# Batch 0 of x loaded and folded whole, the first half of w_in loaded in quarters, and the odd DFT units ahead of the even ones

## The chip, the cores and the metric

The kernel runs on one core of one Trainium2 chip. The metric is the time on the device in microseconds (us), the median of several executions. The kernel before took 1268.69 us (3 runs, 1268.38 to 1270.33). All runs told here gave correct results, and all their profiled executions were of the fast state, with a mean granted TensorE clock of 0.986 to 0.996.

Engines: PE is TensorE (PEld its weight loads), DVE is VectorE, ACT is ScalarE, POOL is GpSimd, SP is SyncE, which only issues DMAs here. SPq and ACTq are the queues in which SP and ACT issue them.

## The reference

```python
def reference(x, w_in, conv_w, w_out):          # x: 8 x 3136 x 256; w_in: 256 x 1024; w_out: 1024 x 256
    x = np.fft.fft(np.fft.fft(x, axis=1), axis=2).real.astype(np.float32)
    h = np.maximum(x @ w_in, 0.0)
    # three taps along the sequence, zero padded
    conv_out = sum(conv_w[k] * hp[:, k:k + S, :] for k in range(3))
    return ((h / (1.0 + np.exp(-conv_out))) @ w_out).astype(np.float32)
```

(Shortened.) The weights come as 64-bit floats and are narrowed to 32 bits on DVE.

## The kernel before

The sequence transform is cut down by symmetry. A *fold* on DVE (`pair`, `both`, `feats`, `evens`) adds and subtracts mirrored rows of x and leaves `w`. PE multiplies `w` with two cosine and sine tables in nine *units* (four even, two `odd_even`, two `odd`, one feature unit); each unit is copied from PSUM by ACT and finished by DVE (`fin`) into `pt` and `qt`. The transform along the feature axis is multiplied into w_in: `blocks` makes `G` from w_in and the DFT matrix `dm`. The main loop then makes `pa` and `pb` from `pt`, `qt` and `G`, and `combine` (DVE) starts the gated part. Row `er` is one row that goes by DMA from `qt` to one partition, through the feature unit on POOL, to DRAM (`ed`), and back in four broadcasts (`eb`); ACT *seeds* every `pa` from `eb`.

Only batch 0 has its fold and its transform in the open. For the other seven they are spread over the main loop.

How a weight is narrowed and where its raw bits lie:

```python
    def narrow(dst, raw):                       # seven DVE instructions
        lo, hi = raw[:, :, 0], raw[:, :, 1]
        ts(out=d, in0=hi, scalar1=20, scalar2=0x7FF, op0=lsr, op1=ALU.bitwise_and)
        # ... four more
        stt(out=lof, in0=lo.bitcast(U32), scalar=2.0 ** -32, in1=hi, op0=ALU.mult, op1=ALU.add)
        stt(out=dst, in0=lof, scalar=2.0 ** -20, in1=dst, op0=ALU.mult, op1=ALU.mult)
    class Weight:
        # self.raw = pool.tile([P, c, n, 2], I32, ...)    c: the two row halves t of w_in, n: columns
        def load(self, eng, c=None):
            eng.dma_start(out=self.raw[:, c].rearrange("p c n e -> p c (n e)"), in_=self.src[:, c])
        def narrow(self, c, cols):
            narrow(self.dst[:, c, cols], self.raw[:, c, cols])
```

The order of the head (cut):

```python
    w_cv.load(nc.scalar)
    nc.scalar.dma_start(out=dm, in_=dft_dim[:, :, 0:2])
    # x of batch 0 in two halves of 2 KB pieces, the second held back; then
    load_tables(1)                              # first table; w_in half 0, load_tables(0), w_in half 1 follow
    # ...
    for f in fold_ops(0): f()
    w_out.load(nc.sync)                         # its raw bits take x's buffer
    for par in (1, 0): mend_tables(par, half)   # ACT
    for i, u in enumerate(us[j] for j in (0, 1, 4, 2, 3, 5, 6, 7, 8)):   # 0, 1: odd, sn = 1; 5, 6: odd, sn = 0
        u.matmuls(0, 1); u.copy()               # PE; ACT
        if i == 2: flip()
        u.fin()                                 # DVE
        if i < 2: w_in[0].narrow(i, slice(0, H))
        if i == 1: row()                        # asks for er
        if i == 2: store(); spread(0, range(len(chunks)))   # ed; eb. Then x of batch 1
        if i == 6: blocks(0)
```

(In the list, 0 and 1 are the first `odd_even` and `odd`, 4 is the feature unit, 5 and 6 are the other `odd_even` and `odd`, and 2, 3, 7 and 8 are even.)

## Time and profile before

| | kernel before |
|---|---|
| median | 1268.69 us |
| span and clock of the profiled run | 1265.7 us, 0.994 |
| fold of batch 0 ends, w_out issued | 31.05, 23.05 us |
| `er` asked for, feature unit on POOL done | 47.25, 52.54 us |
| first seed, `combine` 0, `combine` 1 | 59.30, 62.24, 67.86 us |

The page of the profile gives the busy time of each engine as a share of the span, and then one digit per fortieth of the span (9 is 90% busy or more):

```profile
PE 1186.2 (94%) x4878; PEld 891.4 (70%) x4878; DVE 1146.4 (91%) x1739; ACT 885.4 (70%) x1835; POOL 397.9 (31%) x503
...
PE   0877999899999999999999999999999999999998
...
DVE  6499998999999989899899989998999878899996
```

PE is nearly full all along, but for the first slice of 31.6 us, with digit 0. What this change can win lies in and right after it. The prediction shows the other views of this kernel.

### The profile page before, as it was taken

The page shows a single profiled execution, that of the slowest core. Times are in us where ns is not written, and L with a number is a line of the kernel's source. Part 1 is how long each engine was busy: PE and PEld are TensorE (multiplying, and loading weights), DVE is VectorE, ACT ScalarE, POOL GpSimd, SP SyncE. Part 2 cuts the span into 40 slices and gives each one's busy share as a digit, 9 for nine tenths or more (in the row PEclk, how much of TensorE's full clock was granted, in tenths as well). Part 3 has the DMA queues.
Part 4 walks back from the last instruction along what each step waited for, and adds up shares of the span by engine and source line. Part 5 has one row for each costly group of instructions (what it writes and reads, how often), then busy time and mean ns, then how long its engine had stood idle before and what let it go on. Part 6 is the DMA issues. An engine that isn't in the chain of part 4 may idle for free.

```text
span 1265.7 us, 15557 instructions
## 1 busy us (share of the span) xinstructions
PE 1186.2 (94%) x4878; PEld 891.4 (70%) x4878; DVE 1146.4 (91%) x1739; ACT 885.4 (70%) x1835; POOL 397.9 (31%) x503
## 2 busy tenths in 40 slices
PE   0877999899999999999999999999999999999998
PEld 0545677677677767777677777777777777777776
DVE  6499998999999989899899989998999878899996
ACT  1344667677767767777767777776777778788885
POOL 5202642424333234242523324242322213222222
PEclk9988999999999999999999999999999999999999
DMA  9401321202212003020202103020011001010000
GB/s 238 146 16 30 98 77 45 58 28 75 64 58 68 26 22 95 25 84 26 72 24 64 49 26 91 31 83 1 26 45 33 30 26 38 28 29 30 30 26 30
DMA packets 47178, 66.06 MB, mean 52 GB/s; under 512 B 5684, under 2 KB 35276, under 8 KB 47096
## 3 DMA queue, kind: packets, MB, share of 16 engines
q1 hardware_dynamic: 41668, 51.93, 13.5%
q0 software_dynamic: 5120, 12.85, 3.7%
q8 instruction: 39, 0.64, 0.2%
q10 hardware_dynamic: 308, 0.29, 0.1%
q14 instruction: 43, 0.35, 0.1%
HBM read 39.26 MB, written 25.74 MB: 51 GB/s over the span
## 4 chain that ended last, share of the span: by engine, by line
PE 62%; DVE 23%; issue 5%; DMA 4%; ACT 4%; POOL 1%; SPq 0%; DVEq 0%; ACTq 0%; POOLq 0%
PE po L91 38%; PE pb L91 9%; PE pa L91 8%; DVE g L568 7%; PE pd L91 6%; DVE h L556 3%; DVE g L589 3%; DMA tab<-dft_seq_dram 2%; ACT nb L545 2%; DVE xh L158 1%; DVE xh L169 1%; DVE w L185 1%; ACT g L581 1%; DMA er<-qt 1%; DVE w L186 1%
## 5 line engine op out<-in xcount | busy, mean ns | idle before, releaser
L91 PE MATMUL po<-wout,g 128*128 128x256 f32 x3072 | 715.4, 382 | 32.4 <-DVE g L589 28.7
L91 PEld LDWEIGHTS po<-wout,g 128*128 128x128 f32 x3072 | 579.0, 190 | 194.5 <-DVE g L589 71.5
L568 DVE SCALAR_TENSOR_TENSOR g<-h,cw,g 128x770 f32<-128x770 f32 (+1 forms) x512 | 554.8, 1084 | 10.6 <-ACT g L562 1.5
L588 POOL TENSOR_TENSOR g<-g,h 128x385 f32<-128x385 f32 (+1 forms) x256 | 239.2, 935 | 743.5 <-ACT g L581 528.7
L581 ACT ACTIVATE g<-g 128x385 f32<-128x385 f32 (+2 forms) x512 | 244.5, 528 | 222.2 <-DVE g L568 222.0
L545 ACT ACTIVATE nb<-pb 128x386 f32<-128x386 f32 (+2 forms) x484 | 213.6, 494 | 83.0 <-PE pb L91 81.6
L556 DVE CUSTOM_DVE_ANT_0 h<-pa,nb 128x386 f32<-128x386 f32 (+2 forms) x498 | 258.2, 558 | 1.9 <-ACT h L542 1.9
L562 ACT ACTIVATE g<-h,cw 128x770 f32<-128x770 f32 (+1 forms) x256 | 243.6, 952 | 0.2 <-DVE h L556 0.2
L91 PE MATMUL pb<-qt,G 127*128 127x387 f32 (+2 forms) x512 | 213.9, 498 | 0.8 <-ACT nb L540 0.8
L91 PE MATMUL pa<-pt,G 128*128 128x387 f32 (+2 forms) x512 | 212.1, 495 | 0.9 <-ACT pa L513 0.5
L513 ACT ACTIVATE pa<-eb,ge 128x387 f32<-128x387 f32 (+2 forms) x256 | 154.0, 602 | 1.6 <-DVE h L556 1.6
L589 DVE TENSOR_TENSOR g<-g,h 128x385 f32<-128x385 f32 (+1 forms) x256 | 152.0, 594 | 1.2 <-ACT g L581 1.2
L91 PEld LDWEIGHTS pa<-pt,G 128*128 128x128 f32 x512 | 96.6, 189 | 75.4 <-issue 18.7
L91 PE MATMUL pd<-tab,w 99*128 99x196 f32 (+2 forms) x448 | 117.4, 374 | 0.0
L91 PEld LDWEIGHTS pb<-qt,G 127*128 127x128 f32 x512 | 94.0, 190 | 23.4 <-issue 3.5
L133 POOL DMA_INDIRECT xh<-in_x_dram,idx x64 | 98.1, 1533 | 17.9 <-issue 12.4
L91 PEld LDWEIGHTS pd<-tab,w 99*128 99x128 f32 (+1 forms) x448 | 82.9, 190 | 12.8
L608 ACT COPY os<-po 128x256 f32<-128x256 f32 x196 | 58.1, 397 | 10.4 <-PE po L91 5.8
L158 DVE TENSOR_TENSOR xh<-xh 98x1020 f32<-98x1020 f32 (+1 forms) x32 | 45.5, 1421 | 7.4 <-DMA xh<-in_x_dram,idx 7.4
L91 PE MATMUL po<-tab,w 98*128 98x196 f32 (+4 forms) x64 | 18.2, 442 | 26.6 <-ACT tab L223 23.7
L169 DVE TENSOR_TENSOR xh<-xh 98x1024 f32<-98x1024 f32 (+1 forms) x32 | 40.5, 1266 | 0.1
L91 PEld LDWEIGHTS po<-tab,w 98*128 98x128 f32 (+1 forms) x64 | 13.1, 222 | 30.6 <-issue 26.0
(100 smaller groups left out, 398.2 us busy)
## 6 DMA issues: line engine op xcount, KB each, us to landing
out_dram<-os SPq DMA_DIRECT2D x192, 128.0 KB
xh<-in_x_dram SPq DMA_DIRECT2D x16, 784.0 KB
eb<-ed SPq DMA_DIRECT2D x16, 193.5 KB
tab<-dft_seq_dram SPq DMA_DIRECT2D x4, 601.8 KB
raw<-in_moe_w_in_dram SPq DMA_DIRECT2D x2, 1024.0 KB
raw<-in_moe_w_out_dram SPq DMA_DIRECT2D x1, 2048.0 KB
eb<-ed SPq DMA_DIRECT2D x8, 209.0 KB
eb<-ed SPq DMA_DIRECT2D x8, 193.0 KB
```

The source lines that it names most:

```text
L91: nc.tensor.matmul(o, l, r, start=start, stop=stop, skip_group_check=True)
L133: nc.gpsimd.indirect_dma_start(out=xh[b, h][0:NP, 7 - m].rearrange("p q d -> p (q d)"), out_offset=None, in_=bass.AP(tensor=x.tensor, offs ...
L158: vt(a[:, :, :, 1:D], a[:, :, :, 1:D], r[:, :, :, D - 1:0:-1], op=ALU.add)
L513: act(pa[s][:, 0:n], eb[b, c], AF.Copy, scale=ge[:, f:f + 1])
L545: act(nb[s][:, i, cols], p[:, cols], AF.Copy, scale=-1.0 if i else 1.0)
L556: nc.vector._custom_dve(TENSOR_ADD_SAT, out=to, in0=a[:, cols], in1=c[:, i, cols], s0=BIG, s1=0.0)
L562: act(gs[s], hs[s][:, 0:n], AF.Copy, scale=cw[:, 0, s[2]:s[2] + 1])
L568: stt(out=g, in0=h[:, k:k + n], scalar=cw[:, k, f:f + 1], in1=g, op0=ALU.mult, op1=ALU.add)
L581: act(gs[s][:, c], gs[s][:, c], AF.Sigmoid)
L588: gt(g[:, p], g[:, p], h[:, p], op=ALU.mult)
L589: vt(g[:, v], g[:, v], h[:, v], op=ALU.mult)
L608: nc.scalar.copy(out=osb[:, j % 2], in_=pt[:, j % 2])
```

## The change

It has three parts, all in that head. Batch 0 of x comes in 4 KB pieces into one tile and is folded whole instead of in two halves. w_in is narrowed in quarters of 256 columns (quarters 0 and 1 come in one load each, quarters 2 and 3 in one together), and quarter 0 is loaded ahead of x, so that its narrowing and `blocks(0)` are done while x is on its way. The two odd units with sn = 0 go ahead of the even ones, and the mend of the second table is put off until they are through, so that nothing waits for that table. w_out's raw bits now lie in x's single tile, so its load follows the whole fold.

```diff
-    xp = ctx.enter_context(tc.tile_pool(name="xp", bufs=2))
+    xp = ctx.enter_context(tc.tile_pool(name="xp", bufs=1))
@@ class Weight
-        def load(self, eng, c=None):
-                eng.dma_start(out=self.raw[:, c].rearrange("p c n e -> p c (n e)"), in_=self.src[:, c])
+        def load(self, eng, cols=None):
+                eng.dma_start(out=self.raw[:, :, cols].rearrange("p c n e -> p c (n e)"),
+                              in_=self.src[:, :, 2 * cols.start:2 * cols.stop])
@@ loads
+    w_in[0].load(nc.sync, quarter(0))
     w_cv.load(nc.scalar)
+    zero(0, 0, nc.scalar)
     nc.scalar.dma_start(out=dm, in_=dft_dim[:, :, 0:2])
+    for m in (0, 2):
+        plain(0, 0, nc.sync, m, m + 2)
+    for m in range(4):
+        mirrored(0, 0, m)
+    load_tables(1)
+    w_in[0].load(nc.sync, quarter(1))
+    load_tables(0)
+    w_in[1].load(nc.sync)
@@ compute
     w_cv.narrow(0, slice(0, P))
+    narrow_in(0)                       # t = 0 and t = 1 of quarter 0
     for f in fold_ops(0):
         f()
     w_out.load(nc.sync)
-    for par in (1, 0):
-        mend_tables(par, half)
+    blocks(0)
+    mend_tables(1, half)
-    for i, u in enumerate(us[j] for j in (0, 1, 4, 2, 3, 5, 6, 7, 8)):
+    for i, u in enumerate(us[j] for j in (0, 1, 5, 6, 4, 2, 3, 7, 8)):
+        if i == 4:
+            mend_tables(0, half)
```

(Cut: the functions that address x, the other quarters, the loop that places them, and a part: ahead of `blocks(0)`, PE now multiplies the DFT matrix into the two `pa` buffers, with results that nothing reads. Before, `blocks(0)` itself used these buffers.)

More of the change, by code (lines that the diff above doesn't have):

```diff
@@ L95, in spare @@
         return pso.tile([P, 2, D], F32, name="po", tag="po").rearrange("p a d -> p (a d)")
-    xh, wt, ea = {}, {}, {}
-    idx = const.tile([P, 1], I32, name="idx")
-    nc.gpsimd.iota(idx, pattern=[[0, 1]], base=2 * (NP - 1), channel_multiplier=-2,
-                   allow_small_or_imprecise_dtypes=True)
-    sg = const.tile([P, 2, 2], F32, name="sg")
+    xt = xp.tile([P, 8, HQ, D], F32, name="xh", tag="xh")
+    wt, ea = {}, {}
+    idx = [const.tile([P, 1], I32, name="idx%d" % i) for i in range(2)]
@@ L105 @@
+    for i in range(2):
+        nc.gpsimd.iota(idx[i], pattern=[[0, 1]], base=(1 + i) * (NP - 1), channel_multiplier=-1 - i,
+                       allow_small_or_imprecise_dtypes=True)
+    sg = const.tile([P, 2, HQ], F32, name="sg")
     nc.gpsimd.memset(sg[:, 0], -1.0)
     nc.gpsimd.memset(sg[:, 1], 1.0)
-    def hold(t):
-        nc.gpsimd.memset(t[0:1, 0, 0, 0:1], 0.0)
-    def load_ops(b, h, eng, held=False):
-        def plain():
-            t = xp.tile([P, 8, 2, D], F32, name="xh", tag="xh")
-            xh[b, h] = t
-            if held:
-                hold(t)
-            eng.dma_start(out=t[0:NP, 0:4], in_=bass.AP(
-                tensor=x.tensor, offset=x.offset + (b * S + 1 + 2 * h) * D,
-                ap=[[HQ * D, NP], [Q4 * D, 4], [1, 2 * D]]))
-        def zero():
-            t = xh[b, h]
-            for s0, n, r in ((0, 4, 0), (4, 3, 1), (7, 1, 0)):
-                eng.dma_start(out=t[NP:KR, s0:s0 + n], in_=bass.AP(
-                    tensor=x.tensor, offset=x.offset + (b * S + r * Q4) * D,
-                    ap=[[D, 1], [Q4 * D, n], [0, 2], [1, D]]))
-        def mirrored(m):
-            def f():
-                nc.gpsimd.indirect_dma_start(
-                    out=xh[b, h][0:NP, 7 - m].rearrange("p q d -> p (q d)"),
-                    out_offset=None,
-                    in_=bass.AP(tensor=x.tensor, offset=x.offset,
-                                ap=[[2 * D, B * S // 2], [1, 2 * D]]),
-                    in_offset=bass.IndirectOffsetOnAxis(ap=idx[0:NP, 0:1], axis=0),
-                    element_offset=(b * S + (4 - m) * Q4 - HO + 2 * (1 - h)) * D)
-            return f
-        return [plain] + [zero] * h + [mirrored(m) for m in range(4)]
@@ L143, in fold_ops, with place, plain @@
-    def fold_ops(b):
-        def half(h):
-            k = slice(0, NP if h == 0 else KR)
-            qs = slice(2 * h, 2 * h + 2)
-            def t():
-                return xh[b, h]
+    def place(b, h):
+        if b == 0:
+            return slice(0, HQ), slice(0, HQ)
+        n = HQ // 2
+        return slice(n * h, n * (h + 1)), slice(n * (1 - h), n * (2 - h))
+    def plain(b, h, eng, m0=0, m1=4):
+        qs, sl = place(b, h)
+        eng.dma_start(out=xt[0:NP, m0:m1, sl].rearrange("p s q d -> p s (q d)"), in_=bass.AP(
+            tensor=x.tensor, offset=x.offset + (b * S + m0 * Q4 + 1 + qs.start) * D,
+            ap=[[HQ * D, NP], [Q4 * D, m1 - m0], [1, (qs.stop - qs.start) * D]]))
@@ new lines, in zero, with mirrored @@
+    def zero(b, h, eng):
+        qs, sl = place(b, h)
+        for s0, n, r in ((0, 4, 0), (4, 3, 1), (7, 1, 0)):
+            q = sl if b == 0 else slice(sl.start, sl.start + 1) if s0 else slice(sl.stop - 1, sl.stop)
+            eng.dma_start(out=xt[NP:KR, s0:s0 + n, q], in_=bass.AP(
+                tensor=x.tensor, offset=x.offset + (b * S + r * Q4) * D,
+                ap=[[D, 1], [Q4 * D, n], [0, q.stop - q.start], [1, D]]))
+    def mirrored(b, h, m):
+        qs, sl = place(b, h)
+        n = qs.stop - qs.start
+        nc.gpsimd.indirect_dma_start(
+            out=xt[0:NP, 7 - m, sl].rearrange("p q d -> p (q d)"),
+            out_offset=None,
+            in_=bass.AP(tensor=x.tensor, offset=x.offset,
+                        ap=[[n * D, B * S // n], [1, n * D]]),
+            in_offset=bass.IndirectOffsetOnAxis(ap=idx[HQ // n - 1][0:NP, 0:1], axis=0),
+            element_offset=(b * S + (4 - m) * Q4 - HO + HQ - qs.stop) * D)
@@ L155, in pair, with load_ops, part @@
+    def load_ops(b, h):
+        return ([lambda: plain(b, h, nc.sync)] + [lambda: zero(b, h, nc.sync)] * h +
+                [lambda m=m: mirrored(b, h, m) for m in range(4)])
+    def fold_ops(b):
+        def part(h):
+            qs, sl = place(b, h)
+            k = slice(0, KR if qs.stop == HQ else NP)
+            xs = xt[k, :, sl]
             def pair(m):
                 def f():
-                    a, r = t()[k, m:m + 2], t()[k, 7 - m:5 - m:-1, ::-1, :]
+                    a, r = xs[:, m:m + 2], xs[:, 7 - m:5 - m:-1, ::-1, :]
@@ L158, in f @@
                     vt(a[:, :, :, 1:D], a[:, :, :, 1:D], r[:, :, :, D - 1:0:-1], op=ALU.add)
                     if m == 2:
-                        a, r = t()[k, 0:4], t()[k, 7:3:-1, ::-1, :]
+                        a, r = xs[:, 0:4], xs[:, 7:3:-1, ::-1, :]
                         vt(a[:, :, :, 0], a[:, :, :, 0], r[:, :, :, 0], op=ALU.add)
@@ L164, in flat @@
             def flat(i, j):
-                return t()[k, i:j].rearrange("p s q d -> p (s q d)")
+                return xs[:, i:j].rearrange("p s q d -> p s (q d)")
             def both(to, op):
@@ L182, in f @@
                     w, s = wt[b][odd], 6 * odd
-                    v = t()[k, s:s + 2]
+                    v = xs[:, s:s + 2]
                     lo, hi = v[:, :, :, 1:P], v[:, :, :, D - 1:P:-1]
@@ L188, in f @@
                     if odd:
-                        gt(w[k, 2:4, qs, P - 1], t()[k, 7:5:-1, :, P], sg[k], op=ALU.mult)
+                        gt(w[k, 2:4, qs, P - 1], xs[:, 7:5:-1, :, P], sg[k, :, 0:qs.stop - qs.start], op=ALU.mult)
                     else:
@@ L195, in half @@
                     feats(0)]
-        return half(0) + half(1)
+        return part(0) if b == 0 else part(0) + part(1)
     tabs = [const.tile([P, n, HQ, HE], F32, name="tab%d" % n) for n in (2, 4)]
@@ L418, with __init__ @@
     class Weight:
-        def __init__(self, dst, src, pool, tag):
+        def __init__(self, dst, src, raw):
             self.dst, self.src = dst, src
-            k, c, n = dst.shape
             self.raw = None
             if src.dtype != F32:
-                self.raw = pool.tile([P, c, n, 2], I32, name="raw", tag=tag)[0:k]
+                self.raw = raw([P, *dst.shape[1:], 2])[0:dst.shape[0]]
                 self.src = src.bitcast(I32)
-        def load(self, eng, c=None):
-            c = slice(0, self.dst.shape[1]) if c is None else slice(c, c + 1)
+        def load(self, eng, cols=None):
+            cols = slice(0, self.dst.shape[2]) if cols is None else cols
             if self.raw is None:
-                eng.dma_start(out=self.dst[:, c], in_=self.src[:, c])
+                eng.dma_start(out=self.dst[:, :, cols], in_=self.src[:, :, cols])
             else:
-                eng.dma_start(out=self.raw[:, c].rearrange("p c n e -> p c (n e)"), in_=self.src[:, c])
+                eng.dma_start(out=self.raw[:, :, cols].rearrange("p c n e -> p c (n e)"),
+                              in_=self.src[:, :, 2 * cols.start:2 * cols.stop])
         def narrow(self, c, cols):
@@ L440 @@
     make_identity(nc, ident)
-    dm = gp.tile([P, 2, 2, P], F32, name="dm", tag="g")
     cw24 = gp.tile([3 * NF, 1, P], F32, name="cw24", tag="g")
@@ L447, with quarter @@
     H = F // 2
+    wout = const.tile([P, NF, D], F32, name="wout")
     win = [pqp.tile([P, NK], F32, name="win", tag=tag)[:, 0:F].rearrange("p (t n) -> p t n", t=2)
            for tag in ("pt", "qt")]
-    w_cv = Weight(cw24, moe_conv_w.rearrange("k (m p) -> (k m) p", m=NF).unsqueeze(1), gp, "g")
-    w_in = [Weight(win[i], moe_w_in[:, i * H:(i + 1) * H].rearrange("(t p) n -> p t n", p=P), wp, "w%d" % i)
-            for i in range(2)]
+    w_cv = Weight(cw24, moe_conv_w.rearrange("k (m p) -> (k m) p", m=NF).unsqueeze(1),
+                  lambda sh: gp.tile(sh, I32, name="raw", tag="g"))
+    w_in = [Weight(win[i], moe_w_in[:, i * H:(i + 1) * H].rearrange("(t p) n -> p t n", p=P),
+                   lambda sh: wp.tile(sh, I32, name="raw", tag="w%d" % i)) for i in range(2)]
+    dm = gp.tile([P, 2, 2, P], F32, name="dm", tag="g")
+    w_out = Weight(wout, moe_w_out.rearrange("(c p) o -> p c o", p=P),
+                   lambda sh: xt[:, 0:NF, 0:2].rearrange("p c q d -> p c (q d)").bitcast(I32)
+                   .rearrange("p c (n e) -> p c n e", e=2))
+    def quarter(i):
+        return slice(i % 2 * H // 2, (i % 2 + 1) * H // 2)
+    w_in[0].load(nc.sync, quarter(0))
     w_cv.load(nc.scalar)
+    zero(0, 0, nc.scalar)
     nc.scalar.dma_start(out=dm, in_=dft_dim[:, :, 0:2])
-    ops = load_ops(0, 0, nc.sync)
-    for f in ops:
-        f()
-    plain, zero, *mirrored = load_ops(0, 1, nc.sync, held=True)
-    plain()
-    zero()
-    for f in mirrored[0:2]:
-        f()
-    hold(tabs[1])
-    for f in mirrored[2:4]:
-        f()
-    load_tables(1)
-    for i in range(2):
-        if w_in[i].raw is not None and i == 0:
-            hold(w_in[i].raw)
-        w_in[i].load(nc.sync)
-        if i == 0:
-            load_tables(0)
-    wout = const.tile([P, NF, D], F32, name="wout")
+    for m in (0, 2):
+        plain(0, 0, nc.sync, m, m + 2)
+    for m in range(4):
+        mirrored(0, 0, m)
+    nc.gpsimd.memset(tabs[1][0:1, 0, 0, 0:1], 0.0)
+    load_tables(1)
+    w_in[0].load(nc.sync, quarter(1))
+    load_tables(0)
+    w_in[1].load(nc.sync)
     G = const.tile([P, 2, F], F32, name="G")
@@ L479, in blocks @@
     def blocks(i):
+        w, n = win[i // 2][:, :, quarter(i)], H // 2
         for g in range(2):
-            p = spare() if i else psa.tile([P, 512], F32, name="pa", tag="pa")
+            p = spare()
             for t in range(2):
-                mm(p, dm[:, t, g, :], win[i][:, t], t == 0, t == 1)
-            nc.scalar.copy(out=G[:, g, i * H:(i + 1) * H], in_=p)
+                mm(p[:, 0:n], dm[:, t, g, :], w[:, t], t == 0, t == 1)
+            nc.scalar.copy(out=G[:, g, i * n:(i + 1) * n], in_=p[:, 0:n])
         p = spare()
-        for m in range(NF // 2):
+        for m in range(NF // 4):
             for t in range(2):
-                mm(p[:, m:m + 1], win[i][:, t, m * P:(m + 1) * P], dm[:, t, 1, P - 1:P], t == 0, t == 1)
-        nc.scalar.copy(out=ge[:, i * NF // 2:(i + 1) * NF // 2], in_=p[:, 0:NF // 2])
+                mm(p[:, m:m + 1], w[:, t, m * P:(m + 1) * P], dm[:, t, 1, P - 1:P], t == 0, t == 1)
+        nc.scalar.copy(out=ge[:, i * NF // 4:(i + 1) * NF // 4], in_=p[:, 0:NF // 4])
     def taps():
@@ L611, in mm2, with narrow_in @@
         gs.pop(s)
+    def narrow_in(i):
+        for t in range(2):
+            w_in[i // 2].narrow(t, quarter(i))
     w_cv.narrow(0, slice(0, P))
+    narrow_in(0)
     for f in fold_ops(0):
         f()
-    w_out = Weight(wout, moe_w_out.rearrange("(c p) o -> p c o", p=P), xp, "xh")
     w_out.load(nc.sync)
     taps()
-    for par in (1, 0):
-        mend_tables(par, half)
+    for g in range(2):
+        mm(psa.tile([P, 512], F32, name="pa", tag="pa"), dm[:, 0, g, :], dm.rearrange("p t g i -> p (t g i)"),
+           True, True)
+    blocks(0)
     begin, us, row, flip, store = units(0)
@@ L625 @@
     nc.gpsimd.memset(PQ[0][1][96:P, :], 0.0)
-    for i, u in enumerate(us[j] for j in (0, 1, 4, 2, 3, 5, 6, 7, 8)):
+    mend_tables(1, half)
+    for i, u in enumerate(us[j] for j in (0, 1, 5, 6, 4, 2, 3, 7, 8)):
+        if i == 4:
+            mend_tables(0, half)
         u.matmuls(0, 1)
         u.copy()
-        if i == 2:
-            flip()
-        u.fin()
-        if i < 2:
-            w_in[0].narrow(i, slice(0, H))
-        if i == 1:
-            row()
-        if i == 2:
+        u.fin()
+        if i == 1:
+            narrow_in(1)
+            row()
+        if i == 4:
+            flip()
             store()
             spread(0, range(len(chunks)))
-            for f in load_ops(1, 0, nc.sync):
+            for f in load_ops(1, 0):
                 f()
-        if i == 6:
-            blocks(0)
     steps = [(b, c, f) for b in range(B) for c in range(len(chunks)) for f in range(NF)]
@@ L650, in at @@
         side.setdefault((cycle, where), []).append(fn)
-    for i in range(4):
-        at(i // 2, "dve", lambda i=i: w_in[1].narrow(i // 2, slice(i % 2 * H // 2, (i % 2 + 1) * H // 2)))
-    at(1, "pe", lambda: blocks(1))
+    for i in (2, 3):
+        for t in range(2):
+            at(2 * i - 4 + t, "dve", lambda i=i, t=t: w_in[1].narrow(t, quarter(i)))
+        at(2 * i - 3, "pe", lambda i=i: blocks(i))
     for c in range(NF):
         at(1 + c, "dve", lambda c=c: w_out.narrow(c, slice(0, D)))
-    for j, fn in enumerate(load_ops(1, 1, nc.sync)):
+    for j, fn in enumerate(load_ops(1, 1)):
         at(NF + 1 + j // 3, "load", fn)
@@ L675 @@
                 c1 = cs[7 * h + 6] + 1
-                for j, fn in enumerate(load_ops(b + 1, h, nc.sync)):
+                for j, fn in enumerate(load_ops(b + 1, h)):
                     at(c1 + (j + 1) // 2, "load", fn)
@@ L704 @@
     copies(steps[0])
+    blocks(1)
     for t in range(n + LAG):
```

## The prediction

The sum is: 0 to 1 us from the worked chain, 2.5 us put off, 1268.7 - 2.5 = 1266.2 us. What the trace before does show: seven packets are under way at once in 92% of the 35 to 39 us, w_out's last packet ends at 47.61 us, and `er`'s three packets of 2092 B run from 48.63 to 48.87 us. The "1.3 us to landing" is an estimate: from the last packet to the instruction that waited it took 1.20 us for the second half of x (22.18, 23.38), 1.06 and 0.57 us for the two tables (28.28, 29.34; 39.75, 40.32) and 0.35 us for `er` (48.87, 49.22).

> **What bounds the kernel now.** I asked first where the time is lost at all: the table of busy times by stretch. Its columns are the stretch, then busy time (and instruction count) of PE, PEld, DVE, ACT and POOL, the granted clock, the DMA share and GB/s.
>
> ```profile
> 20.00:30.00 10.00, 0.00 (x0) 0.00 (x0) 6.63 (x10) 0.66 (x1) 1.47 (x3) 1.00 1.00 246
> ...
> 34.00:38.00 4.00, 4.00 (x10) 3.05 (x10) 0.00 (x0) 0.00 (x0) 0.00 (x0) 1.00 0.42 167
> ...
> 80.00:90.00 10.00, 8.92 (x30) 5.18 (x29) 9.65 (x17) 7.32 (x14) 1.84 (x3) 1.00 0.00 1
> ...
> 900.00:1200.00 300.00, 299.49 (x1251) 229.83 (x1249) 274.76 (x404) 234.41 (x489) 73.73 (x99) 1.00 0.09 28
> ```
>
> From 80 us on DVE, later PE, is full: the 1200 us of the main loop can only be moved as a block. The head, until the first `combine` at 62.24 us, is half empty, and the change works there. Second, the chain of waits restricted to the head (start, length, what):
>
> ```profile
> 16.32 23.92 DMA tab<-dft_seq_dram
> ...
> 40.32 0.94 ACT tab L223
> ...
> 49.68 0.91 DVE raw L415
> ...
> 50.61 0.91 DVE win L416
> ...
> 51.57 2.84 PE pa L91 x6
> 54.41 4.61 PE po L91 x32
> ...
> 59.44 0.51 DVE pt L274
> ```
>
> The chain waits for the second cosine/sine table until 40.3 us, then for w_in's narrowing, then PE's `blocks(0)` (two pieces, 7.45 us with the last even units), then the last even unit. Third, the timelines of ACT, DVE, POOL and the SP queue, for what waited beside that chain:
>
> ```profile
> 30.32 3.28 ACT L227 ACTIVATE tab<-tab 99x784 f32<-99x784 f32 x4
> 40.32 0.94 ACT L223 ACTIVATE tab<-tab,half 2x786 f32<-2x786 f32 x1 [6.72 <-DMA tab<-dft_seq_dram]
> ```
> ```profile
> 41.64 0.36 DVE L293 TENSOR_TENSOR as<-as,po 128x196 f32<-128x196 f32 x1 [10.59 <-ACT as L289]
> ```
> ```profile
> 49.33 0.72 POOL L336 TENSOR_TENSOR er<-as 1x197 f32<-1x197 f32 x1 [16.77 <-DMA er<-qt]
> ```
> ```profile
> 47.25 0.73 SPq L345 DMA_DIRECT2D er<-qt  x1
> 52.57 0.27 SPq L352 DMA_DIRECT2D ed<-er  x1
> 53.90 1.76 SPq L362 DMA_DIRECT2D eb<-ed  x4
> ```
>
> DVE idles 10.6 us because ACT's copy of the first unit sits behind the mend of the second table. And there is a second chain, nearly as late: row `er` (47.25, usable 49.2), POOL's feature unit to 52.54, `ed` to DRAM, four broadcasts `eb`. The packets of the first broadcast end near 57.2 us; with about 1.3 us to landing it is usable near 58.5, and the first seed starts at 59.30. So the table's chain beats it by less than 1 us.
>
> Last, the DMA view of 35 to 39 us:
>
> ```profile
> DMA packets 122, 0.70 MB, mean 175 GB/s; under 512 B 9, under 2 KB 9, under 8 KB 122
> ...
> q1 hardware_dynamic: 122, 0.70, 43.8%
> ```
>
> 43.8% is 7 of 16 engines, each busy.
>
> [...]here the odd unit's 392-column matmuls start 0.65 us apart before 39.7 us and 0.33 us after.
>
> Packet records: a 2048 B packet takes 84 ns when the engines run undisturbed and about 130 ns when x, tables and weights mix; 4096 B 159 and about 255; 6288 B 242 and about 410. Per byte it is the same for 2 and 4 KB: mixed about 16 GB/s per engine, undisturbed 25. POOL's mirrored loads of x already travel mostly as 4096 B packets.
>
> **The change part by part.**
>
> *x in 4 KB pieces.* Eight indirect issues become four (0.97 us each), done by about 7 instead of 13.4 us, so x comes first and whole. By the rates above the longer packet saves nothing of the transfer. Ahead of pair(2) must land x 3.2, w_in quarter 0.5, DFT matrix 0.26 MB: 4.0 MB. Before, 2.0 MB had moved by 10.0 us; the rest at 250 GB/s takes 8 us; plus 1.3 us to landing: 19.3 us (second half before: 23.4).
>
> *Folded whole.* 1020 elements cost 1.22 us, 508 cost 0.69: 1.04 ns per element plus 0.16 us. Whole: pair 2.2, pair 2.4, both 2.2, feats 2.3, both 2.2, evens 2.3, feats 2.3. From 19.3 us the odd features are ready at 26.2 (27.3 before), the fold ends at 33.0 (31.05 before). Fewer fixed costs, but no early half: no gain.
>
> *w_in in quarters.* One narrowing of 128x256 takes 2.57 us (62.80 to 65.37). Quarter 0 (5.1 us) falls into DVE's idle 6 to 11 us, and blocks(0) leaves the path. Quarter 1 (5.1 us) lies where two 512-wide ones (7.9 us) lay; quarters 2 and 3 cost DVE the same four narrowings in the loop.
>
> *Odd units first, mend(0) late.* The table wait at 40.3 leaves the path. What starts the units is the first table. [...]so I take 29.7. No gain there; mended (4.2 us) at 34.
>
> From 34 us: odd_even(1) with a cold PE to 36.4, odd(1) to 41, its fin at 42.2, narrowing to 47.3, odd_even(0) and odd(0) fins to 48.9, even units, limited by `po` buffers, to 53. Products could start at 53 instead of 60: up to 7 us.
>
> **The second chain takes it back.** Row `er` is now asked for at 42.2[...]. [...]So `er` is usable at about 48.7, POOL ends at 51.9 (3.2 us), and the first `eb` lands 6 us later as before, 57.9: seed at 58 instead of 59.3. Then pa and its extra product 1.4 us, ACT and `combine(0)` near 60.6 (before 62.24), a gain of 1.6. PE then does blocks(1) (8 matmuls of 256 columns, 8 of one: about 2.6 us) before products of step 1, so `combine(1)` comes near 65.1 with DVE idle about 1.5 us; before it came at 67.86 with one narrowing (2.57 us) more done, which is worth 65.3. **Sum: about 0 to 1 us from the worked chain**, and 7 us if `er` came as early as it is asked for. I put 2.5 us off: the mixing rates are my weakest figures and an orderly x should mix rather less than two halves interleaved with tables.
>
> **Rivals.**
> 1. *x arrives at the undisturbed rate.* For: plain x alone shows 84 ns per 2 KB. Against: from 10.5 us, almost alone, it takes 130. x would land near 16[...]: 3 us or more, 1262 to 1264.
> 2. *`er` isn't held by w_out*, because w_out, issued only at the fold's end, [...]falls behind `er`. Then products start at 53 to 55: 1262.
> 3. *The fold becomes the bound*: pair(2) slips to 22 us with tables interleaved; fold ends at 36 and DVE is late for odd fins: 1269 to 1271.
> 4. *One x tile makes false waits in the loop*, half-loads waiting for the wrong half. Against: ACT's strided write of `er` (49.22) and POOL's (49.33) overlap in time, so waits follow the elements, not the range. If wrong, 7 batches lose 1 us or more each: 1275 and up. Few per cent.
>
> **Range and chances.** 1268.7 - 2.5 = 1266.2 us. Rivals 1 and 2 together give 1261, rival 3 gives 1270.5: that is my range. Two per cent is 25 us, nearly all that lies empty between 31 and 62 us, and no step reaches it: faster 0.01, same 0.98, slower 0.01.
>
> **What would show it.** Pair(2) of batch 0 at 19 us, the first mend at 30, first odd fin near 37; no ACT wait for the second table in front of the first copy; POOL's first feature operation waiting for the `er` DMA until about 48.7; first seed near 58 waiting for `eb`, not for ACT's copy; DVE idle about 1.5 us ahead of the second combine; after 125 us both traces alike but for a shift. POOL's `er` operation far below 47 us would refute the main term; first `combine` below 57 us would make the prediction wrong on the fast side, and longer waits for x loads in the loop on the slow side.

## The result

The changed kernel took **1274.49 us** (median of 4 runs, 1273.54 to 1275.48), the kernel before 1269.16 (4 runs) beside it: ratio 1.0041, 95% interval 1.0024 to 1.0059. By the 2% measure that is "same", but it is slower, and 4.0 us above the top of the predicted range. A ratio is always the mean time of one kernel's fast runs over that of the other's of the same rounds, so it is not quite the ratio of the medians.

Busy times by stretch of the changed kernel (stretch, length, then PE, PEld, DVE, ACT, POOL with counts, granted clock, DMA share, GB/s):

```profile
20.00:30.00 10.00, 4.63 (x6) 1.85 (x6) 0.71 (x3) 0.00 (x0) 0.00 (x0) 1.00 0.52 184
30.00:40.00 10.00, 4.43 (x14) 3.81 (x14) 9.79 (x11) 4.29 (x8) 1.23 (x2) 1.00 0.65 188
...
900.00:1200.00 300.00, 299.45 (x1252) 229.59 (x1251) 273.74 (x406) 233.73 (x485) 74.47 (x100) 1.00 0.09 28
```

The loop is the same as before (299.45 us of PE in 300 us; before 299.49). The head is not: DVE was busy 6.63 us between 20 and 30 us, now it is busy for 0.71. What it does there is in its timeline (start, length, engine, line, operation, and in brackets the idle time before it and who ended it):

```profile
5.54 0.34 DVE L414 TENSOR_SCALAR win<-raw 128x256 int32<-128x256 int32 x1 [0.37 <-DMA raw<-in_moe_w_in_dram]
...
7.87 0.43 DVE L421 SCALAR_TENSOR_TENSOR win<-raw,win 128x256 f32<-128x256 f32 x1
29.22 0.29 DVE L414 TENSOR_SCALAR win<-raw 128x256 int32<-128x256 int32 x1 [20.93 <-DMA raw<-in_moe_w_in_dram]
...
31.45 0.43 DVE L421 SCALAR_TENSOR_TENSOR win<-raw,win 128x256 f32<-128x256 f32 x1
31.80 2.28 DVE L163 TENSOR_TENSOR xh<-xh 99x2040 f32<-99x2040 f32 x1
```

The first half of quarter 0 is narrowed at 8.2 us. The second half, the same seven instructions on the other row half of the same quarter, starts at 29.22, after 20.93 us of idling for a DMA of w_in. The fold is behind it in DVE's program, and all of it ran later: pair(0), which reads x, at 31.80 (in e1, told below, where this wait is gone, at 15.88). Which DMA that was is told by the queue of SP:

```profile
0.74 0.46 SPq L437 DMA_DIRECT2D raw<-in_moe_w_in_dram  x1
1.26 0.99 SPq L120 DMA_DIRECT2D xh<-in_x_dram  x2
7.17 1.78 SPq L218 DMA_DIRECT2D tab<-dft_seq_dram  x2
...
16.06 0.40 SPq L437 DMA_DIRECT2D raw<-in_moe_w_in_dram  x1
...
28.08 0.39 SPq L437 DMA_DIRECT2D raw<-in_moe_w_in_dram  x1
48.14 0.37 SPq L437 DMA_DIRECT2D xh<-in_moe_w_out_dram  x1
50.72 0.72 SPq L350 DMA_DIRECT2D er<-qt  x1
58.43 0.27 SPq L357 DMA_DIRECT2D ed<-er  x1
59.76 1.76 SPq L367 DMA_DIRECT2D eb<-ed  x4
```

There are three loads of raw bits: quarter 0 at 0.74 us, quarter 1 at 16.06, half 1 at 28.08. Quarter 0 had landed by 5.54, when its first half was narrowed; the third had only just been issued. So it waited for quarter 1, of which it reads nothing. All that follows is late: w_out (at the fold's end) at 48.14 (before, where it didn't wait for the whole fold, 23.05; in e1, told below, where it does, 38.85), `er` at 50.72 instead of 47.25, `ed` and `eb` at 58.43 and 59.76.

The timeline of ACT and its queue:

```profile
1.44 4.73 ACTq L129 DMA_DIRECT2D xh<-in_x_dram  x3
8.93 0.64 ACTq L472 DMA_DIRECT2D dm<-dft_dim_dram  x1
...
36.40 0.16 ACT L500 COPY ge<-po 128x2 f32<-128x2 f32 x1 [1.13 <-PE po L91]
36.59 0.95 ACT L228 ACTIVATE tab<-tab,half 2x786 f32<-2x786 f32 x1
```

The first of POOL's four feature operations:

```profile
56.25 0.54 POOL L341 TENSOR_TENSOR er<-as 1x197 f32<-1x197 f32 x1 [6.68 <-DMA er<-qt]
```

And DVE's first two `combine`:

```profile
66.88 0.56 DVE L564 CUSTOM_DVE_ANT_0 h<-pa,nb 128x385 f32<-128x385 f32 x1 [4.69 <-ACT h L550]
...
72.68 0.56 DVE L564 CUSTOM_DVE_ANT_0 h<-pa,nb 128x385 f32<-128x385 f32 x1 [2.68 <-ACT h L550]
```

The DFT matrix is issued at 8.93, behind the zero rows of x, whose three issues took 4.73 us from 1.44 on (before, without them in front, at 1.42), and PE waits for it until 24.91; `blocks(0)` ends behind the late narrowing, and with it ACT's copies of `G`, in front of the mend of the first table (36.59, though that table was there: in a run told below its mend starts at 30.09). POOL waits for `er` until 56.25. The second `combine` comes at 72.68. Before, it came at 67.86 with one more narrowing (2.57 us) done ahead of it, so 65.29 is its like: 7.4 us later. The span is 7.9 us longer.

Part of the 7.4 us arises behind the seed. PE stands still for 2.72 us ahead of it, and the granted clock is 0.50 between 66 and 68 us: two matmuls on `pa` take 1.27 us instead of 0.81, and `blocks(1)` 3.17 instead of 1.89. From the first seed (63.60) to `combine` 1 it takes 9.1 us, against 7.4 in e1, e2 and a1.

### The profile page after: what moved, and what is told of

The parts are those of the page before. It is cut to its first block, busy times and chain, and to the rows that moved or that the text cites. A ratio compares the mean times of both kernels' runs of the same rounds, so it can differ in the third digit from the quotient of the medians.

```text
span 1273.6 us, 15551 instructions
## 1 busy us (share of the span) xinstructions
PE 1192.2 (94%) x4898; PEld 898.3 (71%) x4898; DVE 1147.9 (90%) x1742; ACT 885.9 (70%) x1841; POOL 390.5 (31%) x494
## 5 line engine op out<-in xcount | busy, mean ns | idle before, releaser
L136 POOL DMA_INDIRECT xh<-in_x_dram,idx x60 | 93.1, 1552 | 16.9 <-issue 12.5
L163 DVE TENSOR_TENSOR xh<-xh 98x1020 f32<-98x1020 f32 (+2 forms) x30 | 45.2, 1508 | 0.0
L174 DVE TENSOR_TENSOR xh<-xh 98x1024 f32<-98x1024 f32 (+2 forms) x30 | 40.2, 1342 | 0.0
L192 POOL COPY w<-xh 98x4 f32<-98x4 f32 (+2 forms) x30 | 24.2, 805 | 42.2 <-DVE xh L174 36.4
L279 DVE TENSOR_TENSOR qt<-as,pd 128x197 f32<-128x197 f32 (+1 forms) x14 | 7.2, 518 | 24.9 <-ACT as L275 24.9
```

What stands on the lines that cost most here:

```text
L136: nc.gpsimd.indirect_dma_start(out=xt[0:NP, 7 - m, sl].rearrange("p q d -> p (q d)"), out_offset=None, in_=bass.AP(tensor=x.tensor, offset ...
L163: vt(a[:, :, :, 1:D], a[:, :, :, 1:D], r[:, :, :, D - 1:0:-1], op=ALU.add)
```

## The experiments

The theory after the reading: the second narrowing of quarter 0 waits by mistake, because the rows of quarter 0 and quarter 1 alternate in the raw tile. The first rival: the DFT matrix, issued late, holds the chain. Further questions were what the parts of the change are worth without that wait, and whether `er` is held up by w_out, as predicted.

All were timed in 5 rounds. All outputs are right. There were three calls, each on another chip, with these medians of the kernel before: 1268.94 (9 runs, one of them an outlier of 3212.79 us, which isn't a fast run), 1270.49 and 1269.39 us (11 each). The table puts all together. "Shift" is `combine` 1 against the kernel before, 65.29 us for those kernels that have w_in in quarters, 67.86 for the others.

| run | what | median, us | ratio to before [95%] | first seed | `combine` 1 | shift | span minus 1265.7 |
|---|---|---|---|---|---|---|---|
| changed kernel | | 1274.49 | 1.0041 [1.0024, 1.0059] | 63.60 | 72.68 | +7.4 | +7.9 |
| a1_dm_only | changed, DFT matrix first | 1274.70 | 1.0043 [1.0027, 1.0060] | 65.22 | 72.61 | +7.3 | +7.2 |
| e1_raw_by_quarter | changed, raw tile by quarters | 1266.96 | 0.9984 [0.9969, 0.9998] | 55.77 | 63.16 | -2.1 | -1.7 |
| e2_dm_first | e1 and DFT matrix first | 1264.17 | 0.9962 [0.9948, 0.9976] | 54.74 | 62.14 | -3.2 | -3.3 |
| e2_again | the same | 1264.12 | 0.9955 [0.9939, 0.9971] | 55.66 | 63.05 | -2.2 | -2.2 |
| e7_old_order | e2, old order of units | 1264.21 | 0.9962 [0.9943, 0.9981] | 54.29 | 61.69 | -3.6 | -3.7 |
| e3_wout_after_row | e2, w_out after `er` | 1264.54 | 0.9965 [0.9951, 0.9979] | 56.03 | 63.54 | -1.8 | -1.6 |
| e5_wout_after_spread | e2, w_out after `eb` | 1267.57 | 0.9971 [0.9955, 0.9987] | 55.12 | 62.52 | -2.8 | +1.8 |
| e4_tab_after_x | e5, first table after x | 1271.23 | 1.0006 [0.9990, 1.0023] | 56.33 | 63.73 | -1.6 | +2.3 |
| e6_x_halves | e2, x in halves | 1269.40 | 0.9995 [0.9980, 1.0010] | 55.74 | 64.83 | -0.5 | -0.3 |
| b1_odd_first | before, new order alone | 1265.39 | 0.9978 [0.9964, 0.9992] | 57.01 | 65.58 | -2.3 | -2.3 |
| b3_x_whole | before, x whole alone | 1266.14 | 0.9969 [0.9954, 0.9984] | 57.43 | 65.99 | -1.9 | -1.9 |
| b4_odd_first_x_whole | before, both | 1272.00 | 1.0019 [1.0003, 1.0035] | 62.91 | 71.47 | +3.6 | +3.6 |

The last two columns agree within 0.6 us in all but e5 and e4: what the head gains or loses, the span gains or loses, and the loop only moves. So an experiment can be read at `combine` 1. (Profiled run and median differ by up to 2 us, and a gain of 1 us is at the edge of what these runs tell.)

### e1_raw_by_quarter: the raw tile by quarters

```diff
-   self.raw = raw([P, *dst.shape[1:], 2])                      # [P, t, n, 2]
+   self.raw = raw([P, parts, c, n // parts, 2])                # w_in half 0: [P, quarter, t, n/2, 2]
-   eng.dma_start(out=self.raw[:, :, cols]..., in_=...)
+   eng.dma_start(out=self.raw[:, self.part(cols)]..., in_=...)
-   narrow(self.dst[:, c, cols], self.raw[:, c, cols])
+   narrow(self.dst[:, c, cols], self.raw[:, self.part(cols), c])
```

The same DMAs, the same bytes, the same instructions, in the same order; only where they lie in the tile differs. In the list of waits of the built program, the first instruction of the second narrowing waits for quarter 1's DMA in the changed kernel, and for nothing here.

> The changed kernel with w_in's raw tile laid out quarter by quarter, so that the second narrowing of quarter 0 no longer carries the wait for the landing of quarter 1 (29.2 us in the changed kernel's trace); every DMA, its order and every other wait stay. Theory (the false wait holds back DVE and the fold behind it): that narrowing starts at 8.2 us, pair(2) of batch 0 near 25 us instead of 34, fold ends near 39 instead of 48; the units then start near 37.5 us, when ACT has mended the first table, since ACT still waits for the DFT matrix (24.9 us) through blocks(0); first seed near 58.7 instead of 63.6; about 5 us off the changed kernel: 1269 to 1270 us, level with before. Rival A (x itself lands late, near 31 us): no change, 1274.5. Rival B (w_out in front of row er alone holds the head back): the first seed follows er, and with w_out now issued at 39 us er lands in 1.5 us after it is asked for.

DVE's timeline, the lines that answer to those of the changed kernel:

```profile
7.87 0.43 DVE L421 SCALAR_TENSOR_TENSOR win<-raw,win 128x256 f32<-128x256 f32 x1
8.21 0.29 DVE L414 TENSOR_SCALAR win<-raw 128x256 int32<-128x256 int32 x1
...
15.88 2.28 DVE L163 TENSOR_TENSOR xh<-xh 99x2040 f32<-99x2040 f32 x1 [5.01 <-DMA xh<-in_x_dram,idx]
24.70 2.28 DVE L163 TENSOR_TENSOR xh<-xh 99x2040 f32<-99x2040 f32 x1 [6.54 <-DMA xh<-in_x_dram,idx]
```

The second narrowing follows the first at 8.21, and DVE reaches pair(0) at 15.88 instead of 31.80. The time is 1266.96 us, about 7.5 us below the changed kernel, and the first seed comes at 55.77 (58.7 had been expected). The false wait is the loss. That x isn't there for pair(2) until 24.70 is the next thing to see.

### a1_dm_only: the DFT matrix first, the false wait left in

```diff
-    zero(0, 0, nc.scalar)
     nc.scalar.dma_start(out=dm, in_=dft_dim[:, :, 0:2])
+    zero(0, 0, nc.scalar)
```

> The change with only the DFT matrix moved ahead of the zero rows; the raw tile, and with it the second narrowing's wait for quarter 1, stays. Theory (the false wait is the main cause, the late DFT matrix a second one): the second narrowing still starts near 29 us, pair(0) near 32, the fold ends near 48, first seed 62.5 to 63.6, time 1272.5 to 1274.5. Rival (the late DFT matrix and the G copies behind it cost most of it): seed near 59, time near 1269 or below.

DVE's timeline:

```profile
30.51 0.29 DVE L414 TENSOR_SCALAR win<-raw 128x256 int32<-128x256 int32 x1 [22.18 <-DMA raw<-in_moe_w_in_dram]
...
33.08 4.47 DVE L163 TENSOR_TENSOR xh<-xh 99x2040 f32<-99x2040 f32 x2
```

The wait is there as before, to 30.51, and the time is 1274.70 us: nothing gained. The rival, that the late DFT matrix holds the chain, is out for the changed kernel.

### e2_dm_first, e2_again: both mends

The edit of a1 on top of e1.

> As e1_raw_by_quarter, and the DFT matrix ahead of the zero rows on ACT's queue[...] (issued at 8.9 us, landed 24.9 in the changed kernel). Theory: blocks(0) runs near 11 us, ACT mends the first table as soon as it lands (about 27.5 us, done at 32), the units start at about 32.5 us, first seed near 54.5: another 4 us off e1, 1265 to 1266 us. Rival (the DFT matrix is off the path, the odd features bind): no more than 1 us off e1.

> The mended kernel once more, for the same rounds as the others: 4 to 5 us below the kernel before, as in the first call (4.8).

The timeline of PE where it first needs the DFT matrix, and of ACT up to the first mend:

```profile
15.78 3.78 PE L91 MATMUL pa<-dm 128*128 128x512 f32 x4 [9.87 <-DMA dm<-dft_dim_dram]
```

```profile
22.45 0.16 ACT L506 COPY ge<-po 128x2 f32<-128x2 f32 x1 [0.41 <-PE po L91]
30.09 0.94 ACT L228 ACTIVATE tab<-tab,half 2x786 f32<-2x786 f32 x1 [7.48 <-DMA tab<-dft_seq_dram]
```

With the false wait gone the same edit pays: by the ratios 0.9984 and 0.9962 it is 0.22%, 2.8 us. PE has the matrix at 15.78 instead of 24.91, ACT is free at 22.6, and the mend waits for nothing but the first table, at 30.09 (predicted 29.7). The kernel beats both, on two chips: 1264.17 and 1264.12 us, 0.38 and 0.45% below the kernel before.

### e7_old_order: the mended kernel with the old order

```diff
-    mend_tables(1, half)
-    for i, u in enumerate(us[j] for j in (0, 1, 5, 6, 4, 2, 3, 7, 8)):
-        if i == 4:
-            mend_tables(0, half)
+    for par in (1, 0):
+        mend_tables(par, half)
+    for i, u in enumerate(us[j] for j in (0, 1, 4, 2, 3, 5, 6, 7, 8)):
```

(And flip, store and spread move with the units.)

> The mended kernel (quarter-major raw tile, DFT matrix first) with the old order of the units and both mends ahead of them. Theory (order part is worth about 3 us, as it was alone on the kernel before, 3.5): first copy of a unit waits again in ACT for the second table's mend near 39 us, first seed near 57 to 58, time 3 us above the mended kernel of the same call. Rival (w_in in quarters and the late w_out bring the gain by themselves; POOL and er set the end): time within 1 us of the mended kernel.

ACT at the second mend and the first copy of a unit, then DVE at the end of the fold:

```profile
38.83 0.95 ACT L228 ACTIVATE tab<-tab,half 2x786 f32<-2x786 f32 x1 [5.74 <-DMA tab<-dft_seq_dram]
39.80 0.32 ACT L294 COPY as<-po 128x196 f32<-128x196 f32 x1
```

```profile
37.94 1.21 DVE L191 TENSOR_TENSOR w<-xh 99x1016 f32<-99x1016 f32 x1
40.15 0.36 DVE L298 TENSOR_TENSOR as<-as,po 128x196 f32<-128x196 f32 x1 [1.00 <-ACT as L294]
```

The rival was right: 1264.21 against 1264.12 us in the same rounds. ACT does wait for the second table, until 38.83, and copies the first unit at 39.80; but the whole fold keeps DVE busy until 39.15 anyway (37.94 and 1.21), and its idle time is 1.00 us. The new order removes a wait that the whole fold covers.

### b1_odd_first: the new order alone

```diff
-    for par in (1, 0):
-        mend_tables(par, half)
+    mend_tables(1, half)
@@
-    for i, u in enumerate(us[j] for j in (0, 1, 4, 2, 3, 5, 6, 7, 8)):
+    for i, u in enumerate(us[j] for j in (0, 1, 5, 6, 4, 2, 3, 7, 8)):
+        if i == 4:
+            mend_tables(0, half)
```

(And flip, store and spread move with the units.)

> The kernel before with nothing but the new order of units and the second table's mend moved behind four of them. The prediction's claim (the second chain takes back what the odd-first order gives, since er stays behind w_out until about 47.5 us): DVE's wait of 10.6 us goes, row er is asked for near 42 us instead of 47.25 but lands at about 49 as before; 0 to 2 us off before, 1267 to 1269. Rival (er isn't held): er lands near 44 us and the time falls by 4 to 6 us, 1263 to 1265.

POOL's first feature operation:

```profile
48.76 0.54 POOL L336 TENSOR_TENSOR er<-as 1x197 f32<-1x197 f32 x1 [15.60 <-DMA er<-qt]
```

With x in halves, DVE's first `fin` comes at 36.67 instead of 41.64, after 5.02 us of idling instead of 10.59, and `er` is asked for at 42.29. Yet it is usable only at 48.76: w_out, issued at 23.39, stands in front of it in SP's queue (in e3, with w_out issued behind it, `er` was there by 45.04). That is what the prediction said (48.7). What it had not seen is that POOL's four operations are now shorter, 2.1 instead of 3.2 us. Before, they ran beside the narrowing, whose last two instructions read two operands from SBUF. In the trace before, a POOL operation took 0.99 and 1.05 us beside these two, and 0.54 to 0.60 here, where DVE was idle or took one operand from PSUM; these two took 0.90 us each beside POOL (at 49.68 and 50.61) and 0.69 where POOL was idle (at 44.82 and 45.55). The part brings 0.22%, 2.8 us, where 0 to 2 were expected.

### b3_x_whole and b4_odd_first_x_whole: x whole, without and with the new order

b3 takes over all that the change does to x and its fold, and w_out's place in x's tile; w_in stays in halves and `blocks(0)` late. b4 adds b1's edit.

> The kernel before with nothing but x of batch 0 in 4 KB pieces, folded whole, in one tile. Theory: x lands at 23 to 25 us as in halves, the fold ends 7 us later than before (38 to 39 instead of 31), which the old order hides because the second table lands at 40; w_out leaves at 39 instead of 23; time 1266 to 1270, the same as before within 0.2%. Rival (one tile for x brings false waits into the loop): 1273 or more.

> The kernel before with two parts of the change, the new unit order (3.5 us alone) and x of batch 0 whole (4.3 us alone); w_in stays in halves, blocks(0) late. Theory (both work on the same wait: each lets er or the table come earlier, and the units cannot start before the first table near 30 us): less than the sum, 4.5 to 6 us below before. Rival (the gains are of different waits and add): 7.5 to 8 us below before.

The two parts bring 0.31 and 0.22% alone. b3 was expected within 0.2% of the kernel before: with w_out later, the second table is mended from 38.64 instead of 40.32, and the first `fin` comes at 39.97 instead of 41.64. Together the parts cost 0.19%. b4's DVE, at the end of the fold and of the second narrowing, and then its PE:

```profile
38.06 1.21 DVE L190 TENSOR_TENSOR w<-xh 99x1016 f32<-99x1016 f32 x1
...
49.11 0.90 DVE L420 SCALAR_TENSOR_TENSOR win<-raw,win 128x512 f32<-128x512 f32 x1
```

```profile
45.70 1.67 PE L91 MATMUL po<-tab,w 99*128 99x197 f32 x8 [1.07 <-DVE qt L311]
50.60 2.98 PE L91 MATMUL po<-tab,w 99*128 99x196 f32 x8 [3.23 <-DVE as L299]
53.38 4.60 PE L91 MATMUL pa<-win,dm 128*128 128x512 f32 x8
```

In b1 the fold is over at 31.65, so DVE has done the first 512-column narrowing by 41.2 and is through with both and with the next `fin` by 46.7. With x whole it is in the fold until 39.3, and the two narrowings end at 50.0. PE stands still for 3.23 us, until DVE's `fin` at 50.2 gives a PSUM buffer back. By then its clock has fallen: granted 0.50 between 50 and 54 us. `blocks(0)` takes 4.60 us instead of 3.60 in b1, and the last even unit comes behind it. Neither theory expected a loss. This is a fold that becomes the bound, rival 3 of the prediction, and what the quarters are for: in e2 DVE has 5.1 us to narrow at this point, not 9, and `blocks(0)` is long done.

### e6_x_halves: the mended kernel with x in halves

The loads, the fold and the w_out buffer of the kernel before put back into e2 (a long edit of the same functions as in b3, the other way round).

> As e2_dm_first, but x of batch 0 in two halves of 2 KB pieces, folded half by half, as before. Theory (the whole x is the part of the change that gains nothing): fold ends near 33 us instead of 39, units start with the mend at about 34, w_out goes out near 22 us and holds er until about 48.5; time within 1.5 us of e2, 1263 to 1265.5. Rival (4 KB pieces are worth something): 1266 or more.

POOL's first feature operation:

```profile
48.88 0.53 POOL L337 TENSOR_TENSOR er<-as 1x197 f32<-1x197 f32 x1 [17.30 <-DMA er<-qt]
```

The same operation of POOL in e2, and in its second profiled run (e2_again):

```profile
47.32 0.74 POOL L341 TENSOR_TENSOR er<-as 1x197 f32<-1x197 f32 x1 [6.63 <-ACT as L333]
```

```profile
48.40 0.55 POOL L341 TENSOR_TENSOR er<-as 1x197 f32<-1x197 f32 x1 [6.76 <-DMA er<-qt]
```

PE around the first seed in e6:

```profile
52.12 0.81 PE L91 MATMUL pb<-qt,G 127*128 127x386 f32 x2
56.38 1.53 PE L91 MATMUL pa<-pt,G 128*128 128x386 f32 x2 [3.45 <-ACT pa L523]
```

The fold ends at 30.1 instead of 39.1, and it doesn't help: w_out is issued at 24.41, and `er`, asked for at 42.13, is usable at 48.88. In e2 POOL starts at 47.32, when ACT's copies are done, and `er` was there; but in e2_again it waits for `er` until 48.40, hardly less than here. Its first seed (55.66) is as late as e6's (55.74), and still its `combine` 1 comes 1.8 us earlier (63.05 and 64.83). So against that run what e6 loses lies behind the seed: PE stands still for 3.45 us (1.14 in e2_again) and comes back at half clock (0.50 between 57 and 59 us). Its first two matmuls on `pa` take 1.53 us instead of 0.92, the next two 1.49 instead of 0.81, and `blocks(1)` 2.37 instead of 1.89.

Folding whole, where the prediction saw "no gain", is worth 2 to 3 us by the shift and 4 to 5 by the ratios here. That w_out, issued later, keeps out of `er`'s way would explain it in e2, but not in e2_again. No run moves w_out alone in a kernel with halves, so the cause stays open.

### e3_wout_after_row, e5_wout_after_spread, e4_tab_after_x: moving the transfers

```diff
     for f in fold_ops(0):
         f()
-    w_out.load(nc.sync)
@@ e3
             row()
+            w_out.load(nc.sync)
@@ e5
             spread(0, range(len(chunks)))
+            w_out.load(nc.sync)
@@ e4: e5, and the first table made to wait for x
-    nc.gpsimd.memset(tabs[1][0:1, 0, 0, 0:1], 0.0)
+    nc.gpsimd.tensor_copy(tabs[1][0:1, 0, 0, 0:1], xt[0:1, 4, 0, 0:1])
```

> As e2_dm_first, and the load of w_out behind row er on SP's queue. Theory of the prediction[...]: in e2 er lands about 4 us after it is asked for, here within 2 us; first seed 0.5 to 1 us earlier, 1264.5 to 1265.5 us. Rival (er is bound by the odd unit that makes it, not by w_out): no change from e2.

> As e2_dm_first, with the load of w_out issued after the four broadcasts eb, so that neither er nor ed nor eb has it in front (in e3_wout_after_row er landed early, POOL ended at 47.6 instead of 49.7 us, but ed then waited 3.8 us behind w_out instead of 1.3). Theory (the er, ed, eb chain binds and w_out is what delays it): the four broadcasts are issued near 49 us instead of 51.0 (e2), first seed near 52.7 or at the end of the even units (about 53.5) instead of 54.7; 1 to 2 us off e2: 1262.5 to 1263.5. Rival (the even units and PE's half clock after the gap bind): no change, 1264.

> As e5_wout_after_spread, and POOL's write that holds the first table back reads the last mirrored piece of x, so the table is issued only once x has landed. Theory (in the changed kernel x lands at 24 to 25 us instead of the predicted 19.3[...]): pair(2) starts near 19 us, fold ends near 33 instead of 39, the table lands 0 to 2 us later than in e5[...]; time within 1 us of e5, as the mend then binds. Rival (x is slow by itself, as its mirrored half is generated by POOL): pair(2) stays at 23 us or later and the table comes later by 5 us: 1268 or more.

The queue of SP in e3, and DVE in e5 and in e4:

```profile
47.62 0.27 SPq L357 DMA_DIRECT2D ed<-er  x1
51.38 1.76 SPq L367 DMA_DIRECT2D eb<-ed  x4
```

```profile
68.92 0.29 DVE L414 TENSOR_SCALAR wout<-xh 128x256 int32<-128x256 int32 x1 [3.28 <-DMA xh<-in_moe_w_out_dram]
```

```profile
18.70 4.48 DVE L163 TENSOR_TENSOR xh<-xh 99x2040 f32<-99x2040 f32 x2 [7.89 <-DMA xh<-in_x_dram]
```

And in e4 the copy on POOL that waits for the last mirrored piece of x:

```profile
19.31 1.72 POOL L484 COPY tab<-xh 1x1 f32<-1x1 f32 x1 [12.26 <-DMA xh<-in_x_dram,idx]
```

e3: `er`, asked for at 41.81, was there by 45.04, with no w_out in front of it (in b1, with w_out in front, it took from 42.29 to 48.76). POOL was done at 47.6. But between `ed` and `eb` lie 3.76 us instead of 1.3: now `ed` stands behind w_out. That isn't all that ate the gain: the first seed (56.03) follows ACT's copy of the last even unit, not `eb`. PE stood still for 2.98 us, and then the 24 matmuls of the last even units took 7.31 us, against 4.48 in e2 after a gap of 0.49 us. Nothing gained over e2.

e5: the theory was that with w_out out of the way the first seed would come near 52.7. It came at 55.12: POOL starts at 47.16 when ACT's copies are done, as in e2, so w_out wasn't what held the chain there. And w_out after the broadcasts is late for the loop: DVE waits 3.28 us for it. This is most of the 4.6 us by which e5's span departs from its shift; the profiled run was also the slowest of its six (1269.30 us, median 1267.57).

e4 tests the prediction's arrival of x. With the table held back both pairs start from 18.70 back to back, and the copy shows the last of x there at 19.31, the predicted 19.3. With the table beside it, it was 24.7. But the table then lands 3 us later (32.56, e5 29.56), the units start at 36.9 instead of 34.0, and the time is 3.7 us worse, where less than 1 us either way was expected. The fold isn't what the units wait for; the first table is.

## Why the prediction was wrong

The step that failed is this sentence: "Quarter 0 (5.1 us) falls into DVE's idle 6 to 11 us, and blocks(0) leaves the path." Half of quarter 0 did; the other half waited until 29.22 us for quarter 1. A quarter is columns 0 to 255 of both row halves, and the raw tile holds row half 0, then row half 1. The DMA of quarter 1 therefore writes a stretch that begins before and ends behind quarter 0's second piece without touching it. The wait was as if it went by the stretch: 20.93 us here, and none in e1, where each quarter is one stretch. The prediction had thought of this kind of thing as rival 4, but for x in the loop, and set it aside with "waits follow the elements, not the range", read from two engines' strided writes of `er`. That reading didn't carry over to a DMA into the raw tile. e1 takes the wait away and nothing else, and 7.5 us with it. (Rival 4's number, "1275 and up", nearly fits the result, but by chance: it meant x's tile and all the batches, and the loop lost nothing.)

The other steps, one by one:

- *The x transfer, "19.3 us".* 24.7 in e1, 25.1 in e3. "So x comes first and whole" was wrong with the first table, issued from 7.17 us on, beside it. e4 shows the figure right (19.3) when the table is held back. It cost little, since the units wait for the table. How the engines share x was not checked: half of x is issued by POOL, and no view here tells the engines apart.
- *The fold, "ends at 33.0".* 48.0 in the changed kernel, 38.7 in e1: the x transfer's 5.4 us.
- *The first table, "29.7", "mended at 34".* Right without the false wait: 30.09 and 34.4 in e2. In the changed kernel mended at 40.9, behind `blocks(0)` on ACT. That moving `blocks(0)` ahead puts ACT's copies of `G` and the DFT matrix ahead of the units was not counted; the matrix, issued 7.5 us later than before, costs 2.8 us once the false wait is gone and nothing while it is there.
- *"The second chain takes it back."* Right as to `er`, usable at 48.7 behind w_out: 48.76 in b1, 48.88 in e6, 48.40 in e2_again, and by 45.04 in e3, where w_out isn't in front. In the changed kernel w_out itself came so late that it was 56.25 (w_out's packets ran from 49.19 to 55.88, `er`'s three from 55.44 to 55.55). Two terms behind it were too large: POOL's 3.2 us is 2.1 in b1 and 2.4 in e1 without the narrowing beside it, and the 6 us from there to the seed were 5.1 in e1, whose seed came at 55.77 (50.70 and 5.1), not 58.
- *Odd units first.* Worth 2.8 us alone (b1), nothing in the mended kernel (e7), and a loss beside the whole fold without the quarters (b4). The parts do not add.
- *"After 125 us both traces alike but for a shift."* Right: see the two last columns of the table.
- *Rivals 1 to 3.* x didn't arrive undisturbed. `er` held POOL up to 48.40 in e2_again, not in e2 (47.32), and in both products started near 55, as rival 2 says. Rival 3's slip of the fold is there and larger than feared (pair(2) at 24.7, fold to 38.7 in e1, instead of 22 and 36), but not at its cost: e1 and e2 are faster than the kernel before.
- *The clock.* In the 34 to 38 us of the prediction's first view the clock column says 1.00 beside matmuls that take 0.861 us, against 0.492 later. The first clock record in that trace is at 39.68 us; before it the column says nothing. The clock granted was 0.50 after gaps of PE of 2.72 us (changed kernel) and 3.45 us (e6), and from within a gap of 3.23 us on (b4). In e2_again it was 0.50 from 50 to 52 us after a gap of only 1.37 us; from 46 to 50 us PE had been busy for 2.63 of 4 us.

Without the false wait the prediction would have looked good: e1's 1266.96 us against 1266.2. It would have been luck, the late x and DFT matrix against the shorter second chain.

## What to carry to other kernels

When a tile is loaded in pieces by several DMAs, lay each piece out in one stretch; if pieces interleave, look in the list of waits of the built program for an instruction that waits for a load it doesn't read. On DVE such a wait of 20.93 us held back here all that came behind it in the program (the fold ended at 48.0 us, 38.7 in e1), so put early work in front of the main work only if it is sure to be ready. And measure the parts of a change together: two that gain alone can lose in company, and a reordering that removes a wait is worth nothing where other work covers it. Before you explain a difference of 1 to 3 us, look at the granted clock behind every gap of PE: here several such differences were in part a clock of 0.50.
